# Second batch's attention spread over more steps, and a GpSimd drain behind the last gathers

## The chip, the cores and the metric

One core of one Trainium2 chip. The metric is the device time of one execution in microseconds; lower is better. The runs shown of the kernel before have a median of 853.22 us (853.07 to 855.84, 3 runs).

## The reference, cut to what matters

Four batches (b = 0 to 3), 8 heads, 576 positions of 64 features, 32 memory slots. Everything is float32 (the two weights `w_in` and `w_out` come as 64-bit floats).

```python
a = softmax(phi, axis=2)                      # over the 576 positions, per memory slot
k_m, v_m = a^T @ k, a^T @ v                   # 32 memories of each head
attn = softmax(0.125 * q @ k_m^T)             # over the 32 memories
x = merge_heads(attn @ v_m)                   # 2304 rows of 512
h = x @ w_in;  x = (h * sigmoid(h)) @ w_out   # 512 -> 2048 -> 512
# then a mixture of 8 experts, two of them for each row, weighted:
out[row] += weight * (relu(x[row] @ w1[e]) @ w2[e])
```

## The kernel before, in words

The kernel never forms `attn @ v_m`. For each batch it multiplies the memories `v_m` into `w_in` (`project`, L247: one eighth of w_in at a time for batch 0 and 1, two eighths in one call for the later batches and from index 8 on), so that the MLP's first matmul takes the attention weights as its moving operand. A large product is made of three float32r matmuls (high and low parts).

The MLP of all four batches is one list of steps, 32 for each batch (L966 and after). Step s runs `mlp_h` (L275) for one block of 128 hidden features and one of two column tiles (256 or 320 positions): six matmuls into one of two PSUM buffers "h", then tanh on ScalarE (ACT, L286), the product on VectorE (DVE, L288), and the split in high (ACT, L292) and low part (DVE, sometimes GpSimd, L293; L302 for the 64 columns left over). Four steps later `mlp_x` (L310, matmuls in L308) multiplies by w_out. All other work is hung on steps as hooks: `at(step, function, ...)`. The tile scheduler orders the instructions of each engine by the order in which the program names them and by what is ready in its own model; `tc.issue_after(i)` keeps an instruction behind `i` on its engine.

Batch 0's attention is computed ahead of the steps. During its 32 steps (about 33 to 130 us) these hooks run: `fetch_win`/`narrow_win` (turning 64-bit weights into float32 on ACT and DVE, until step 20), `fetch_wout`/`narrow_wout` (on ACT, DVE and GpSimd; block f at step 2f - 1, until step 29), `project(i)` at steps 2, 6, 10, ... 26 and the first call for batch 1, `project(8)`, at step 28; and the whole attention of batch 1:

- `phi_max` (L107), steps 8 and 9, for the two groups of four heads: maximum of phi over the positions (DVE reduction into the tile `mx`, L111, which has one buffer), a transpose on TensorE (PE, L113), a second reduction (L115), a broadcast (L117), subtraction (L120) and exp (L121).
- `memory` (L124), both groups at step 11: 40 small matmuls each (L131), then normalisation into `src` (L133 to L139).
- `memory_t` (L141) at step 14: two transposes and one copy into `kvt`.
- `scores` (L154) at steps 17 and 18, for the two column tiles: 16 matmuls each (L152) and two DVE transposes (L161).
- `softmax_a` (L163) at step 19: maximum (L167), subtraction (L168), exp (L169). `softmax_b` (L172) at step 22: sum (L176), two small instructions (L177, L178), product (L179).
- `split` (L194) at steps 24 and 26: a DVE transpose for each group (L183), high part on ACT (L190), low part on DVE (L191) into the tiles `ah` (three buffers) that `mlp_h` of step 32 reads first.

`phi_max`, `memory`, `memory_t`, `scores` and `project` take their PSUM from one tag, "aux", of two buffers, which are given out in turn; a call that needs one waits until ACT or DVE has read what was in it. `project`'s evictions are L258 (ACT) and L259 (DVE). Batches 2 and 3 do the same during the steps of the batch before them, with both `phi_max` calls ten steps in, and their reduction L111 kept behind the newest L293 on DVE.

Loads are issued by SyncE (SP) in the scheduler's order: phi (L87) goes into the buffer "big", which phi shares with the scores of the batch before; k/v (L97) and q (L105) have four buffers each, which the next batch reuses; the 64-bit weights go through `stage` (L201).

The experts come last (L723): nine parts of up to 640 rows. GpSimd gathers each part's rows by indirect DMA and scatters results into `out` (L716). For a part after the first expert the earlier values of `out` are gathered first (`earlier`, L637, DMAs in L641); for the last part (k = 8) `earlier` is all that GpSimd does ahead of five scatters. At the very end there is a branch over an overflow path (L793), and each engine drains (L1052).

Of the kernel before, what the change touches and what calls it, by code (L numbers as in the profile page):

```python
# [6 lines left out]
F32 = mybir.dt.float32  # L7
# [5 lines left out]
OP = mybir.AluOpType  # L13
AX = mybir.AxisListType

B, H, S, D, M = 4, 8, 576, 64, 32
# [3 lines left out]
SC, NCH = 128, 5  # L20
# [24 lines left out]
def body(ctx, tc, a):  # L45
    nc = tc.nc
    pe, act, dve, pool, sp = nc.tensor, nc.scalar, nc.vector, nc.gpsimd, nc.sync
# [13 lines left out]
    ident = const.tile([128, 128], F32, name="ident")  # L61
# [15 lines left out]
    ap_ = att.enter_context(tc.tile_pool(name="att", bufs=1, side="right"))  # L77
# [24 lines left out]
    def load_q(b, r, t0=0, t1=S):  # L102
        if t0 == 0:
            QT[b, r] = ap_.tile([128, S], F32, name="q", tag="q", bufs=4)
        sp.dma_start(QT[b, r][:, t0:t1], a["qt"][b, r][:, t0:t1])  # L105

    def phi_max(b, g):  # L107
        r = slice(g * 128, (g + 1) * 128)
        mx = ap_.tile([SC, 128], F32, name="mx")
        with tc.issue_after(LATEST[0].ins) if b > 1 else ExitStack():  # L110
            dve.tensor_reduce(mx, PH[b][:, :, r].rearrange("p c j -> p j c"), axis=AX.X, op=OP.max)  # L111
        pt = psum("aux", 2)
        pe.transpose(pt[:, :SC], mx, ident)  # L113
        mt = ap_.tile([128, 1], F32, name="mt")
        dve.tensor_reduce(mt, pt[:, :SC], axis=AX.X, op=OP.max)  # L115
        pb = psum("aux", 2)
        pe.matmul(pb[:SC, :128], mt.to_broadcast([128, SC]), ident, start=True, stop=True)  # L117
        for c0, c1 in ((0, 2), (2, NCH)):
            e = PH[b][:, c0:c1, r]
            dve.tensor_sub(e, e, pb[:SC, None, :128].to_broadcast([SC, c1 - c0, 128]))  # L120
            last = act.activation(e, e, AF.Exp)  # L121
        return last
# [514 lines left out]
    def earlier(k):  # L637
        for j in range(PARTS[k][2]):
            h = height(k, j)
            EX[k, j] = P2["b"].tile([128, DM], F32, name="ex", bufs=CT)[:h]  # L640
            last = pool.indirect_dma_start(out=EX[k, j], out_offset=None, in_=a["out"],  # L641
                                           in_offset=bass.IndirectOffsetOnAxis(ap=GID[k][:h, j:j + 1], axis=0))
        return last
# [79 lines left out]
    def experts(late, last):  # L723
        open_b()
        for k, (e, t0, n) in enumerate(PARTS):
            first, nxt = t0 == 0, k + 1 < len(PARTS)
            new = nxt and PARTS[k + 1][0] != e
            if first:
                for c in range(4):
                    loaded = fetch_w2(e, c)  # L730
            if k == 1:
                gather(2)
                indices(3)
            elif k and nxt:
                with tc.issue_after(puts[-1].ins):
                    g = gather(k + 1, loaded)
                with tc.issue_after(g.ins):
                    g = earlier(k)
                if k + 2 < len(PARTS):
                    with tc.issue_after(g.ins):  # L740
                        indices(k + 2)
            elif k:
                earlier(k)
            for f in range(8):
                up(k, f)
                if k == 0 and f == 2:
                    late(15, 17)
                if k == 0 and f == 4:
                    routed = last(17, 18)
                    split_w2(e, 0)  # L750
                    split_w2(e, 1)
                    table(1)
                    with tc.issue_after(gather(1).ins):
                        table(2)
                        for c in range(2):
                            W1S[1, c] = P2["b"].tile([128, FE], F32, name="w1s", bufs=2)
                            pool.memset(W1S[1, c][:, :1], 0.0)
                            fetch_w1(1, c)
                        for i in range(3, len(PARTS)):
                            table(i)  # L760
                if first and f % 2 and (k or f > 3):
                    split_w2(e, f // 2)
            if nxt:
                flips = iter(range(PARTS[k + 1][2]))
                ahead = PARTS[k + 1][2] - n
                for j in range(max(1, (ahead + 2) // 2) if k else 0):
                    with tc.issue_after(LATEST[0].ins):
                        flip(k + 1, next(flips))
            if new and k > 1:
                for c in range(2):  # L770
                    fetch_w1(e + 1, c)

            for j in range(n) if nxt else (n - 1, *range(n - 1)):
                done = down(k, j, {} if k or j < n - 1 else {10: lambda: flip(1, 0), 18: lambda: flip(1, 1)})
                if nxt and k:
                    for i in range(max(1, (ahead + 2) // 2)):
                        i = next(flips, None)
                        if i is not None:
                            with tc.issue_after(done.ins) if k > 1 else ExitStack():
                                flip(k + 1, i)  # L780
                if new and j < 4:
                    split_w1(e + 1, j)
                    if j < 2:
                        fetch_w1(e + 1, j + 2)
            if new:
                for c in range(n, 4):
                    split_w1(e + 1, c)
                    if c < 2:
                        fetch_w1(e + 1, c + 2)
# [54 lines left out]
        load_q(0, r, T0[1])  # L844
    fetch_wout(0)
    fetch_win(1)
    phi_max(0, 0)
    phi_max(0, 1)
    memory(0, 0)
    memory(0, 1)  # L850
    first = ST.pop(("i", 0))
# [30 lines left out]
    def at(s, fn, *args):  # L882
        hooks.setdefault(s, []).append((fn, args))
# [10 lines left out]
    at(8, routing_setup)  # L894
    for b in range(1, B):
        s = (b - 1) * SB
        o = 2 if b == 1 else 0
        at(s + (1 if b > 1 else 4), load_phi, b)
        for r in range(4):
            at(s + (1 if b > 1 else 5 + r), load_kv, b, r)  # L900
        for r in range(4):
            at(s + (1 if b > 1 else 10), load_q, b, r)
        x = 2 if b > 1 else 0
        at(s + x + 8, phi_max, b, 0)
        at(s + x + 9 - (b > 1), phi_max, b, 1)
        at(s + x + o + 9, memory, b, 0)
        at(s + x + o + 9, memory, b, 1)
        at(s + o + 12, memory_t, b)
        at(s + o + 15, scores, b, 0)
        at(s + o + 16, scores, b, 1)  # L910
        at(s + o + 17, softmax_a, b, 0, S)
        at(s + o + 20, softmax_b, b, 0, S)
        at(s + o + 22, split, b, 0, 0, S)
        at(s + o + 24, split, b, 1, 0, S)
        for i in range(0, NP, 2):
            for x in range(2):
                at(s + SB - 8 + 4 * i, fetch_win, b * NP + i + x)
            at(s + SB - 4 + 4 * i, project, b * NP + i, 2)
# [13 lines left out]
    s = 3 * SB  # L932
# [123 lines left out]
```

## Time and profile before

| | us |
|---|---|
| median of 3 runs | 853.22 |
| the profiled execution | 852.59 |
| its span, first to last instruction | 850.7 |
| TensorE busy | 808.0 |
| VectorE busy | 497.2 |
| ScalarE busy | 361.5 |
| GpSimd busy | 208.6 |

The profile is of one execution. PE is TensorE's matmul, PEld its weight load, DVE VectorE, ACT ScalarE, POOL GpSimd, SP SyncE; a q behind a name is the engine's sequencer (waits, branches, drains, DMA issues), whose time is not counted as busy. Times are counted from the first instruction. TensorE's granted clock was 1.00, 2.4 GHz, in all stretches shown.

### The profile page before, as it was taken

To read this page: it belongs to the slowest core of one execution; us is meant where nothing else is said; L and a number is where in the kernel's file an instruction comes from. 1 tells how busy PE (TensorE), PEld (TensorE's weight loads), DVE (VectorE), ACT (ScalarE), POOL (GpSimd) and SP (SyncE) were. 2 spreads that over 40 slices of the span, in tenths; PEclk is the share of its full clock that TensorE was granted. 3 is DMA by queue.
4 is the path that set the end of the run, shared out by engine and by line. 5 is a ranking of instruction groups with operands and counts; after the bars stand their busy time and mean duration, and the time that the engine had idled before them with its cause. 6 is when DMAs were issued, how large, how long until landed. Compare 5 with 4: busy or idle time off the path is not lost.

```text
span 850.7 us, 14185 instructions
## 1 busy us (share of the span) xinstructions
PE 808.0 (95%) x5260; PEld 691.7 (81%) x5260; DVE 497.2 (58%) x1178; ACT 361.5 (42%) x856; POOL 208.6 (25%) x237
## 2 busy tenths in 40 slices
PE   5588999999999999999999999999999999999994
PEld 2266678778887888887989989989889898898983
DVE  4898996885258757655725555354553545545520
ACT  3688875444344554553413433324333233332410
POOL 0244350021000400500542404115032141331301
PEclk9999999999999999999999999999999999999998
DMA  9899861353064315222456893766748657475201
GB/s 298 282 304 312 301 204 60 111 159 121 1 215 169 51 50 150 58 81 50 112 148 193 249 271 122 157 245 184 210 145 195 236 163 178 176 204 186 73 16 40
DMA packets 85935, 137.84 MB, mean 162 GB/s; under 512 B 14045, under 2 KB 48349, under 8 KB 85856
## 3 DMA queue, kind: packets, MB, share of 16 engines
q1 hardware_dynamic: 74656, 104.41, 40.8%
q0 software_dynamic: 11200, 32.43, 12.4%
q8 instruction: 43, 0.70, 0.4%
q14 instruction: 36, 0.29, 0.1%
HBM read 106.13 MB, written 31.26 MB: 162 GB/s over the span
## 4 chain that ended last, share of the span: by engine, by line
PE 83%; DVE 8%; ACT 3%; issue 2%; DMA 2%; POOL 1%; SPq 0%; POOLq 0%; ACTq 0%
PE x L701 25%; PE x L308 18%; PE x L677 12%; PE h L677 12%; PE h L283 9%; PE aux L152 3%; DVE gl L293 1%; DMA kv<-kv 1%; PE aux L131 1%; POOL wo L227 1%; DVE wo L212 1%; DVE th L288 1%; DMA q<-qt 1%; PE aux L654 1%; ACT lw L206 0%
## 5 line engine op out<-in xcount | busy, mean ns | idle before, releaser
L701 PE MATMUL x<-w,gh 128*128 128x512 f32 (+1 forms) x608 | 188.2, 391 | 0.0
L701 PEld LDWEIGHTS x<-w,gh 128*128 128x128 f32 (+1 forms) x608 | 112.5, 186 | 24.3
L701 PE MATMUL x<-w,gl 128*128 128x512 f32 (+1 forms) x304 | 118.6, 390 | 0.0
L677 PE MATMUL h<-xh,w 128*128 128x304 f32 (+4 forms) x512 | 118.5, 303 | 0.0
L677 PE MATMUL x<-xh,w 128*128 128x304 f32 (+4 forms) x512 | 117.9, 302 | 0.0
L283 PE MATMUL h<-ah,wph 128*128 128x320 f32 (+1 forms) x512 | 108.9, 301 | 3.6 <-DVE th L288 2.0
L308 PE MATMUL x<-gh,woh 128*128 128x512 f32 x256 | 104.8, 410 | 0.0
L283 PEld LDWEIGHTS h<-ah,wph 128*128 128x128 f32 x512 | 90.2, 192 | 17.9 <-ACT ah L190 3.6
L308 PE MATMUL x<-gh,wol 128*128 128x512 f32 x256 | 101.7, 397 | 0.0
L716 POOL DMA_INDIRECT out<-y,tab x40 | 41.6, 1041 | 244.0 <-DVE y L711 189.1
L308 PE MATMUL x<-gl,woh 128*128 128x512 f32 x256 | 100.7, 393 | 0.7 <-DVE gl L293 0.7
L492 POOL DMA_INDIRECT tab_d<-rows,slot x36 | 40.6, 1129 | 194.6 <-DVE slot L489 180.4
L288 DVE SCALAR_TENSOR_TENSOR th<-th,h 128x256 f32<-128x256 f32 (+1 forms) x128 | 57.6, 450 | 52.6 <-ACT th L286 51.9
L677 PEld LDWEIGHTS h<-xh,w 128*128 128x128 f32 x512 | 87.2, 188 | 0.7
L677 PEld LDWEIGHTS x<-xh,w 128*128 128x128 f32 x512 | 87.3, 188 | 0.0
L286 ACT ACTIVATE th<-h 128x256 f32<-128x256 f32 (+1 forms) x128 | 52.2, 408 | 70.8 <-PE h L283 68.3
L677 PE MATMUL x<-xl,w 128*128 128x304 f32 (+4 forms) x256 | 77.9, 304 | 0.0
L677 PE MATMUL h<-xl,w 128*128 128x304 f32 (+4 forms) x256 | 77.7, 303 | 0.0
L283 PE MATMUL h<-ah,wpl 128*128 128x256 f32 (+1 forms) x256 | 76.8, 301 | 0.7 <-DVE wpl L259 0.7
L292 ACT ACTIVATE gh<-th 128x256 fp32r<-128x256 f32 x128 | 53.3, 416 | 55.9 <-DVE th L288 55.7
L293 DVE TENSOR_TENSOR gl<-th,gh 128x256 fp32r<-128x256 f32 x120 | 55.9, 466 | 31.8 <-ACT gh L292 27.9
L711 DVE SCALAR_TENSOR_TENSOR y<-x,tab,ex 128x512 f32<-128x512 f32 (+2 forms) x35 | 26.2, 749 | 71.4 <-PE x L701 71.4
(189 smaller groups left out, 1344.4 us busy)
## 6 DMA issues: line engine op xcount, KB each, us to landing
w2s<-moe_w SPq DMA_DIRECT2D x32, 512.0 KB, 8.1
wi<-win_d SPq DMA_DIRECT2D x24, 512.0 KB, 4.8
w1s<-moe_w SPq DMA_DIRECT2D x24, 512.0 KB, 4.8
kv<-kv SPq DMA_DIRECT2D x16, 520.0 KB, 7.7
st<-moe_w_in SPq DMA_DIRECT2D x16, 512.0 KB, 5.6
st<-moe_w_out SPq DMA_DIRECT2D x16, 512.0 KB, 7.1
xs_d<-ex SPq DMA_DIRECT2D x25, 256.0 KB, 3.6
x_d<-xs SPq DMA_DIRECT2D x36, 128.0 KB, 2.5
```

The source lines that it names most:

```text
L152: pe.matmul(p[g][h * M:(h + 1) * M], KVT[b][r, t, h * M:(h + 1) * M], moving(h)[r], start=True, stop=True)
L283: pe.matmul(p[:, :w], wt[:, g, c:c + 128], AH[b, g][at][:, t0:t0 + w], start=(n == 0), stop=(n == 5))
L286: act.activation(th[:, :w], p[:, :w], AF.Tanh, scale=0.5)
L288: dve.scalar_tensor_tensor(u[:, :w], th[:, :w], 1.0, p[:, :w], op0=OP.add, op1=OP.mult)
L292: act.activation(gh, u[:, :256], AF.Copy)
L293: last = (pool if b == 0 and (2 * f + i) % 4 == 0 else dve).tensor_sub(gl, u[:, :256], gh.bitcast(F32))
L308: pe.matmul(X2[key], held, moved, start=(f == 0 and n == 0), stop=(f == NF - 1 and n == 2))
L492: st = pool.indirect_dma_start(out=tab_d, out_offset=bass.IndirectOffsetOnAxis(ap=slot[:, j, k:k + 1], axis=0), in_=rows.bitcast(I32)[:, j ...
L677: pe.matmul(p[:, :w], wt[:, d, c], x[:, d, r], start=(n == 0), stop=(n == 11))
L701: mm = pe.matmul(p, g, w[:, f, :], start=(n == 0), stop=(n == (15 if both else 23)))
L711: done = dve.scalar_tensor_tensor(y, p[:P], w, EX[k, j], op0=OP.mult, op1=OP.add)
L716: st = pool.indirect_dma_start(out=a["out"], out_offset=bass.IndirectOffsetOnAxis(ap=TAB[k][:P, j, 0:1], axis=0), in_=y, in_offset=None, b ...
```

## The change

Three edits. `phi_max` is cut in two: `phi_top` is the first reduction, in a tile `mx` of two buffers, and `phi_max` the rest. The hooks are placed anew: for batch 1 `phi_top` at 7 and 9, `phi_max` at 9 and 11, `memory` at 12 and 13, `memory_t` at 16, `scores` at 20 and 23, `softmax_a` at 24, `softmax_b` at 25, `split` at 27 and 28; for batches 2 and 3 only `phi_top` moves, to eight and nine steps into the batch before. GpSimd gets a `drain` instruction behind the five gathers of the last part.

```diff
-    def phi_max(b, g):
+    MX = {}
+
+    def phi_top(b, g):
         r = slice(g * 128, (g + 1) * 128)
-        mx = ap_.tile([SC, 128], F32, name="mx")
+        mx = MX[b, g] = ap_.tile([SC, 128], F32, name="mx", bufs=2)
         with tc.issue_after(LATEST[0].ins) if b > 1 else ExitStack():
             dve.tensor_reduce(mx, PH[b][:, :, r].rearrange("p c j -> p j c"), axis=AX.X, op=OP.max)
+
+    def phi_max(b, g):
+        r = slice(g * 128, (g + 1) * 128)
         pt = psum("aux", 2)
-        pe.transpose(pt[:, :SC], mx, ident)
+        pe.transpose(pt[:, :SC], MX.pop((b, g)), ident)
...
             elif k:
-                earlier(k)
+                with tc.issue_after(earlier(k).ins):
+                    pool.drain()
...
-        o = 2 if b == 1 else 0
...
-        x = 2 if b > 1 else 0
-        at(s + x + 8, phi_max, b, 0)
-        at(s + x + 9 - (b > 1), phi_max, b, 1)
-        at(s + x + o + 9, memory, b, 0)
-        at(s + x + o + 9, memory, b, 1)
-        at(s + o + 12, memory_t, b)
-        at(s + o + 15, scores, b, 0)
-        at(s + o + 16, scores, b, 1)
-        at(s + o + 17, softmax_a, b, 0, S)
-        at(s + o + 20, softmax_b, b, 0, S)
-        at(s + o + 22, split, b, 0, 0, S)
-        at(s + o + 24, split, b, 1, 0, S)
+        if b == 1:
+            for step, fn, g in ((7, phi_top, 0), (9, phi_max, 0), (9, phi_top, 1), (11, phi_max, 1),
+                                (12, memory, 0), (13, memory, 1)):
+                at(step, fn, b, g)
+            for step, fn, *more in ((16, memory_t), (20, scores, 0), (23, scores, 1), (24, softmax_a, 0, S),
+                                    (25, softmax_b, 0, S), (27, split, 0, 0, S), (28, split, 1, 0, S)):
+                at(step, fn, b, *more)
+        else:
+            at(s + 8, phi_top, b, 0)
+            at(s + 9, phi_top, b, 1)
+            at(s + 10, phi_max, b, 0)
+            at(s + 10, phi_max, b, 1)
+            at(s + 11, memory, b, 0)
+            at(s + 11, memory, b, 1)
+            at(s + 12, memory_t, b)
...
```

The lines left out at the end are the other hooks of batches 2 and 3, which stay where they were.

## Rows read from the trace of the kernel before

**Rows 1.** The page, busy us of each engine (share of the span) and instructions.

```profile
PE 808.0 (95%) x5260; PEld 691.7 (81%) x5260; DVE 497.2 (58%) x1178; ACT 361.5 (42%) x856; POOL 208.6 (25%) x237
```

**Rows 2.** Busy time by stretch: PE, PEld, DVE, ACT, POOL; then clock, DMA share, GB/s.

```profile
56.50:98.00 41.50, 35.12 (x302) 25.42 (x300) 36.29 (x74) 35.72 (x83) 18.75 (x17) 1.00 0.91 315
...
98.00:111.00 13.00, 13.00 (x84) 10.95 (x83) 12.81 (x25) 11.48 (x27) 4.76 (x5) 1.00 0.85 280
111.00:130.40 19.40, 17.95 (x134) 14.33 (x133) 16.82 (x31) 15.12 (x36) 8.42 (x8) 1.00 0.47 165
...
420.00:840.00 420.00, 419.68 (x2431) 379.66 (x2429) 201.76 (x368) 134.98 (x291) 121.55 (x130) 1.00 0.59 171
```

**Rows 3.** PE's waits, 50 to 131 us: total us, times, longest.

```profile
PE aux L152 <- DVE sct L161: 2.1, 2, 1.4
PE aux L113 <- DVE mx L111: 1.7, 1, 1.7
PE aux L144 <- DVE wpl L259: 1.4, 1, 1.4
```

**Rows 4.** Timeline of DVE: the second batch's two reductions (start, us).

```profile
47.79 1.30 DVE L111 TENSOR_REDUCE mx<-phi 128x128 f32<-128x640 f32 x1
...
60.23 1.23 DVE L111 TENSOR_REDUCE mx<-phi 128x128 f32<-128x640 f32 x1
```

**Rows 5.** Timeline of PE: the same transpose in batches 2 and 3.

```profile
159.69 0.30 PE L113 MATMUL aux<-ident,mx 128*128 128x128 f32 x1 [1.03 <-DVE rows L473]
...
255.06 0.30 PE L113 MATMUL aux<-ident,mx 128*128 128x128 f32 x1 [0.46 <-DVE mx L111]
```

**Rows 6.** Lines L1052, L793 (end) and L1047 (start): ns min/median/max, first and last start.

```profile
L1052 POOLq DRAIN  x3: 46/103/4322, 845.5 to 850.4; - x3
L1052 SPq DRAIN  x3: 7/7/13, 846.2 to 850.1; - x3
...
L793 POOLq INC_SWDGE_SEM  x1: 1235/1235/1235, 844.3 to 844.3; - x1
...
L1047 POOLq INC_SWDGE_SEM  x1: 27/27/27, 0.1 to 0.1; - x1
...
L1047 POOLq DRAIN  x1: 172/172/172, 0.3 to 0.3; - x1
```

**Rows 7.** Groups, 56.5 to 98 us: busy us, mean ns of one, idle before.

```profile
L152 PE MATMUL aux<-q,kvt 64*32 64x256 f32 (+1 forms) x32 | 2.1, 415 | 0.0
...
L161 DVE STREAM_TRANSPOSE sct<-aux 128x256 f32<-128x256 f32 (+1 forms) x4 | 1.9, 474 | 0.2 <-PE aux L152 0.2
```

**Rows 8.** Groups of DVE, 98 to 130.4 us.

```profile
L168 DVE TENSOR_TENSOR sct<-sct,smx 128x1152 f32<-128x1152 f32 x1 | 1.3, 1348 | 0.0
...
L167 DVE TENSOR_REDUCE smx<-sct 128x36 f32<-128x1152 f32 x1 | 1.3, 1341 | 0.0
L176 DVE TENSOR_REDUCE ssm<-sct 128x36 f32<-128x1152 f32 x1 | 1.3, 1339 | 0.0
...
L178 DVE RECIPROCAL ssm<-ssm 128x36 f32<-128x36 f32 x1 | 0.4, 374 | 0.0
L177 DVE TENSOR_SCALAR ssm<-ssm 128x36 f32<-128x36 f32 x1 | 0.2, 176 | 0.0
```

**Rows 9.** Timeline of ACT: the tanh of step 24.

```profile
111.10 0.37 ACT L286 ACTIVATE th<-h 128x256 f32<-128x256 f32 x1
```

**Rows 10.** SP's waits at line L87, the loads of phi (ns min/median/max).

```profile
L87 SPq EVENT_SEMAPHORE  x3: 17/1638/4035, 36.0 to 188.7; - x3
```

**Rows 11.** Timeline of POOL: last gather, first and last scatter of the last part.

```profile
800.38 0.90 POOL L641 DMA_INDIRECT ex<-out,gid  x1 [0.30 <-issue]
819.77 0.94 POOL L716 DMA_INDIRECT out<-y,tab  x1 [18.49 <-DVE y L713]
...
840.75 0.97 POOL L716 DMA_INDIRECT out<-y,tab  x1 [4.46 <-DVE y L711]
```

**Rows 12.** The chain of waits through 38 to 132 us, shares by engine and line.

```profile
by line: DVE gl L293 10.0%; issue 8.9%; PE x L308 8.8%; PE h L283 8.6%; POOL wo L227 7.5%; DVE wo L212 6.2%; DMA q<-qt 5.7%; DVE th L288 4.4%; DVE gc L302 3.3%; PE aux L152 3.2%; ACT lw L206 3.1%; DVE wi L216 3.1%; ACT gh L292 2.9%; ACT wi 
```

More of the change, by code (lines that the diff above doesn't have):

```diff
@@ L105, in load_q @@
         sp.dma_start(QT[b, r][:, t0:t1], a["qt"][b, r][:, t0:t1])
+    MX = {}
+    def phi_top(b, g):
+        r = slice(g * 128, (g + 1) * 128)
+        mx = MX[b, g] = ap_.tile([SC, 128], F32, name="mx", bufs=2)
+        with tc.issue_after(LATEST[0].ins) if b > 1 else ExitStack():
+            dve.tensor_reduce(mx, PH[b][:, :, r].rearrange("p c j -> p j c"), axis=AX.X, op=OP.max)
     def phi_max(b, g):
         r = slice(g * 128, (g + 1) * 128)
-        mx = ap_.tile([SC, 128], F32, name="mx")
-        with tc.issue_after(LATEST[0].ins) if b > 1 else ExitStack():
-            dve.tensor_reduce(mx, PH[b][:, :, r].rearrange("p c j -> p j c"), axis=AX.X, op=OP.max)
         pt = psum("aux", 2)
-        pe.transpose(pt[:, :SC], mx, ident)
+        pe.transpose(pt[:, :SC], MX.pop((b, g)), ident)
         mt = ap_.tile([128, 1], F32, name="mt")
@@ L846, in body @@
     fetch_win(1)
-    phi_max(0, 0)
-    phi_max(0, 1)
+    for g in range(2):
+        phi_top(0, g)
+        phi_max(0, g)
     memory(0, 0)
@@ L902, in body @@
             at(s + (1 if b > 1 else 10), load_q, b, r)
-        x = 2 if b > 1 else 0
-        at(s + x + 8, phi_max, b, 0)
-        at(s + x + 9 - (b > 1), phi_max, b, 1)
-        at(s + x + o + 9, memory, b, 0)
-        at(s + x + o + 9, memory, b, 1)
-        at(s + o + 12, memory_t, b)
-        at(s + o + 15, scores, b, 0)
-        at(s + o + 16, scores, b, 1)
-        at(s + o + 17, softmax_a, b, 0, S)
-        at(s + o + 20, softmax_b, b, 0, S)
-        at(s + o + 22, split, b, 0, 0, S)
-        at(s + o + 24, split, b, 1, 0, S)
+        if b == 1:
[13 more added lines that the diff above has]
+            at(s + 12, memory_t, b)
+            at(s + 15, scores, b, 0)
+            at(s + 16, scores, b, 1)
+            at(s + 17, softmax_a, b, 0, S)
+            at(s + 20, softmax_b, b, 0, S)
+            at(s + 22, split, b, 0, 0, S)
+            at(s + 24, split, b, 1, 0, S)
         for i in range(0, NP, 2):
```

## The prediction

> **What bounds the kernel now.** I read the page's busy times first: TensorE is busy for 808.0 of 850.7 us, VectorE for 497.2 [rows 1]. A gain must come from the 43 us in which TensorE stands still, or from the tail behind its last matmul. The table by stage shows where they are [rows 2]: in 420 to 840 us, the experts, TensorE is busy for 419.68 of 420.00 us, so nothing is to be had there. The first batch's MLP is different. In 56.5 to 98.0 us (about steps 8 to 18) TensorE is busy for 35.12 of 41.5 us and VectorE for 36.29; in the two stretches from 98.0 to 130.4 us (steps 19 to 31) 13.00 + 17.95 and 12.81 + 16.82 of 32.4 us. Both engines are nearly full throughout: that is the fact on which most of this turns.
>
> The waits of TensorE there [rows 3] are of one kind for the most part. The second batch's attention and the projections of w_in share the two PSUM buffers "aux". The transposed memory waits 1.39 us for the eviction of project(4) in front of it in step 14; project(5) waits 2.1 us for the transposes of the first scores. The 1.7 us at the transpose of the second phi maximum come from a tile: `mx` has one buffer, so the reduction of group 1 cannot start before the transpose of group 0 has read it. The first reduction runs at 47.79, the second only at 60.23 us [rows 4]. All waits that lie in 56.5 to 98.0, small ones with them, add up to 41.50 - 35.12 = 6.38 us.
>
> In the later batches the same transpose waits 1.03 and 0.46 us, since the reduction is issued in the step of its reader [rows 5]. At the end, the last scatter is issued at 840.75 us [rows 11], and the program ends 10 us later: GpSimd's INC_SWDGE_SEM starts at 844.3 us (1.235 us), its DRAIN follows and takes 4.322 us [rows 6]. SyncE is at its own drain by 846.3 us [rows 6] and waits.
>
> **The change part by part.** *Second batch, first stretch (steps 8 to 18).* Each pair of "aux" users is now about two steps from the next, and `mx` has two buffers. No arithmetic is added or taken away, and the first batch's own calls keep their order. Both scores leave this stretch: 32 matmuls, 2.1 us of TensorE, and 4 VectorE transposes, 1.9 us [rows 7]. That leaves 35.12 - 2.1 = 33.0 us of TensorE and 36.29 - 1.9 = 34.4 us of VectorE. Of these VectorE is the longer: the stretch can shrink from 41.5 to 34.4 us, by 7.1.
>
> *Steps 19 to 23 (98.0 to 111.0 us).* TensorE had no gap here, 13.00 of 13.00 us [rows 2], and takes in the scores: 13.0 + 2.1 less what their starts overlap, about 14.9 us. VectorE loses five softmax instructions (maximum 1.34, subtraction 1.35, sum 1.34, two small ones 0.37 + 0.18; 4.58 us in all [rows 8]) and has room. This stretch grows by 1.9 us.
>
> *Steps 24 to 31 (111.0 to 130.4 us).* Step 24's tanh is at 111.10 us [rows 9]. VectorE was busy for 16.82 of 19.4 us [rows 2] and gets those 4.58 us: 21.4 us in a stretch that TensorE could do in 17.95. It grows by 2.0 us. The work that stays beside it in VectorE's queue (narrowing w_out, evictions of project(7) and project(8)) waits behind the softmax; w_out's narrowed tiles are needed four to five steps later, which covers them, but the eviction of h is not covered by more than the two "h" buffers. ACT's one exp and two splits move along and lie beside VectorE's work.
>
> Sum for the second batch: 34.4 + 14.9 + 21.4 = 70.7 us against 41.5 + 13.0 + 19.4 = 73.9, a gain of 3.2. This takes each stretch at its longer engine, without waits. By the same rule the kernel before would need 36.29 + 13.0 + 17.95 = 67.2 us and takes 73.9, 10% more; 6.38 of those 6.7 us are the waits that the change pulls apart, so I take the bare rule. Bounds: all of TensorE's idle time in both stretches, 7.8 us, on one side; on the other each stretch keeps VectorE's share of before (87% in the first and the last): 34.4/0.874 + 14.9 + 21.4/0.867 = 79.0, a loss of 5.1.
>
> *Queues that the moves pass.* SyncE's loads for the third batch wait for buffers of the second: phi for the last turn (now two steps later; such a load waits up to 4.0 us [rows 10]), k/v for memory (one or two later), q for the scores (three to five later). Behind them in that queue stand loads of w_out and w_in. The last w_out tiles are narrowed at steps 25 to 29, well behind step 23, so I cost this at nothing, and at up to 2 us if SyncE stays blocked on q until then. By that time the DMA engines' share has fallen from 0.91 to 0.47 [rows 2], which leaves room to catch up.
>
> *Third and fourth batch.* Two reductions of 1.2 us go two and one steps ahead of their readers. TensorE's 1.03 + 0.46 us go. VectorE does the routing's small work there, and 2.5 us of it move behind the reductions; GpSimd, which waits for that routing, has idle time. Bounds: 1.5 us of gain, and none if a reduction is again queued late. I take 1.3.
>
> *The drain.* It is one instruction on GpSimd, behind five gathers that end at 801.3 us; the next instruction there is a scatter that waits for its data until 819.77, after 18.49 us of idleness [rows 11]. A drain of 4.3 us, or one that waits for those gathers to land, is hidden there; were that cover gone, it would hold up the first scatter alone, and four others stand between that and the end. What it does to the last DRAIN no row shows. The rows around it are 172 ns in front of any DMA, and 46 and 103 ns for the two that come right after the long one [rows 6]. Two readings fit: the DRAIN works off something that all the DMAs before it left behind, or it pays for whatever ran last. The first makes the last DRAIN some 0.2 us, with five scatters behind the early one. Then SyncE's end at 846.3 us sets the finish, which comes 0.8 us after it now comes (849.9 to 850.7): 847.1, a gain of 3.6 us. The other end is nothing; a loss is excluded by the 18 us. I take 3.6, because the other three DRAINs, with little or nothing new in front of them, are all short, and five scatters are few beside all that GpSimd issued before. The Trainium skill (VectorE: DVE Perf Modes, The DRAIN you can't avoid) says that the preamble's and postamble's drains take about 12 ns, constant, on all engines; by that the last DRAIN has nothing to give, and the sum would be that of the first rival. GpSimd's 4.322 us disagree with the page.
>
> **Sum.** The profiled execution took 852.59 us (span 850.7). 852.6 - 3.2 - 1.3 - 3.6 = 844.5. The median of the runs shown is 853.22, 0.6 above it, so I forecast 845.1 us.
>
> **Rivals.** *The drain moves nothing.* The last DRAIN pays for INC_SWDGE_SEM just before it, or for the last scatters, and still takes 4.3 us. For it: INC_SWDGE_SEM takes 1.235 us there and 27 ns at the start [rows 6], so the DMAs' bookkeeping may hang on it and not on the drain. Against it: the two later drains are short. Time: 845.1 + 3.6 = 848.7 us.
>
> *The attention moves nothing.* The chain of waits through 38 to 132 us runs over VectorE, ACT and GpSimd more than over TensorE [rows 12]: narrowing the 64-bit weights goes ACT, VectorE, GpSimd, ACT, VectorE. If this chain sets the pace, taking away TensorE's waits only makes it wait for the next tanh. The scheduler may also place the moved work where it was before. Against it: VectorE itself is idle for 5.2 us of the first stretch. With the drain working: 853.2 - 3.6 - 1.3 = 848.3 us; without, 851.9.
>
> *Slower: VectorE's last stretch.* The softmax is squeezed into steps 24 to 28, the attention's halves have to be ready at step 32, and TensorE waits there for evictions of h and for the halves. Its price is the lower bound above, 5.1 us less the 1.3: 853.2 + 3.8 = 857.0 us without the drain's gain. It decides if the first stretch gives back less than the 3.9 us that the other two take. Against it: 111 to 130 us is where VectorE still had 2.6 us idle.
>
> **Chances.** Forecast 0.42; drain moves nothing 0.28; attention moves nothing 0.20 (0.13 with the drain working, 0.07 without); slower 0.10. The range reaches over the forecast and the two rivals at 848: from 842 (3 us of the second batch's upper bound beyond my sum) to 852. Outside lie the slower case and the edges, about 0.2. A measurement of this kernel tells some 0.3%, 2.6 us, from no change, so the cases of 845 and 848 count as faster with a few misses, 0.77; the 851.9 and neighbours as the same, 0.13; slower 0.10.
>
> **What would show it.** TensorE's waits at the memory, its transpose, the scores and both phi transposes gone; steps 8 to 18 near 35 us long, steps 24 to 31 near 21; VectorE close to full in the last. On GpSimd a drain between 801 and 806 us, and the last DRAIN at 0.2 us. I am wrong if the last DRAIN is still 4.3 us, or if TensorE shows new waits for th or ah in steps 24 to 32 of the size of those that went.

## The result, and the profile after

The changed kernel takes 845.51 us (median of 4 runs, 844.75 to 846.22) against 854.53 us of the kernel before beside it (853.07 to 855.88, 4 runs): a ratio of 0.9887, 95% interval 0.9866 to 0.9908. The forecast was 845.1 us in a range of 842 to 852. The profiled execution takes 845.91 us (span 844.1) against 852.59: 6.7 us less, where the medians differ by 9.0. Where the other 2.3 us come from is a finding of its own (below).

First the lead along the program: the start of tanh (ACT) in some steps, the end of the last product y on VectorE, and the end of the span, from the timelines of the two profiled executions.

| | before | after | lead |
|---|---|---|---|
| step 0 | 32.58 | 32.39 | 0.2 |
| step 8 | 58.40 | 58.32 | 0.1 |
| step 19 | 98.83 | 93.69 | 5.1 |
| step 24 | 111.10 | 109.63 | 1.5 |
| step 32 | 131.58 | 129.61 | 2.0 |
| step 48 | 177.13 | 174.20 | 2.9 |
| step 80 | 272.95 | 270.37 | 2.6 |
| step 127 | 385.45 | 382.88 | 2.6 |
| last y ends | 840.47 | 838.35 | 2.1 |
| span ends | 850.71 | 844.13 | 6.6 |

So the second batch gave 2.0 - 0.2 = 1.8 us, the third 0.9, the fourth took 0.4 back, and the end behind the last y shrank from 10.24 to 5.78 us, by 4.46. The 0.4 us between step 127 and the last y belong to the execution and not to the change: in the other profiled executions below that stretch differs from the one of before by 0.0 to +2.1 us, with the attention changed or not.

The page of the changed kernel, busy us of each engine, and its stretches, cut at the same steps as those of [rows 2]:

```profile
PE 807.1 (96%) x5260; PEld 691.4 (82%) x5260; DVE 496.8 (59%) x1178; ACT 360.8 (43%) x856; POOL 209.9 (25%) x237
```

```profile
56.40:92.90 36.50, 35.12 (x284) 27.02 (x282) 32.62 (x67) 33.10 (x80) 17.75 (x17) 1.00 0.92 317
92.90:109.50 16.60, 14.88 (x114) 11.22 (x114) 14.99 (x31) 15.21 (x35) 8.65 (x9) 1.00 0.88 314
109.50:128.40 18.90, 17.61 (x132) 13.79 (x130) 18.22 (x32) 13.19 (x32) 6.76 (x6) 1.00 0.43 155
```

The busy times are those of before, as no work came or went. The three stretches take 72.0 us in place of 73.9 [rows 2]; TensorE stands for 4.39 us in them (1.38 + 1.72 + 1.29), where it stood for 7.83. PE's waits from 50 to 131 us, in the columns of [rows 3], show which ones went and which came:

```profile
PE h L288 <- DVE wpl L264: 2.3, 2, 1.2
PE aux L157 <- DVE wpl L264: 0.7, 1, 0.7
PE aux L122 <- DVE mt L120: 0.7, 1, 0.7
PE h L288 <- DVE th L293: 0.5, 1, 0.5
PE aux L136 <- ACT phi L126: 0.4, 1, 0.4
PE h L288 <- DVE ah L196: 0.3, 1, 0.3
```

The three of [rows 3] are gone. But the waits for `wpl`, the low part of the projected weights, which VectorE evicts, only moved, most of them to h. Before, beside the 1.4 us of [rows 3], there were (lines of the attention and the MLP have moved on by five since: L264 was L259, L288 was L283, L136 was L131):

```profile
PE h L283 <- DVE wpl L259: 0.7, 1, 0.7
PE aux L131 <- DVE wpl L259: 0.7, 1, 0.7
```

So they were 2.8 us before and are 2.3 + 0.7 = 3.0 after. On DVE's timeline the second reduction of phi now follows the first by 3.3 us, where it was 12.4 us [rows 4]:

```profile
47.60 1.30 DVE L113 TENSOR_REDUCE mx<-phi 128x128 f32<-128x640 f32 x1
50.90 1.33 DVE L113 TENSOR_REDUCE mx<-phi 128x128 f32<-128x640 f32 x1
```

At the end, GpSimd's drains and INC_SWDGE_SEM (columns of [rows 6]; L749 is the new drain) and its last DMAs (timeline):

```profile
L749 POOLq DRAIN  x1: 9474/9474/9474, 794.4 to 794.4; - x1
...
L799 POOLq INC_SWDGE_SEM  x1: 300/300/300, 842.3 to 842.3; - x1
...
L1067 POOLq DRAIN  x3: 46/103/464, 842.6 to 843.9; - x3
```

```profile
798.26 0.90 POOL L646 DMA_INDIRECT ex<-out,gid  x1 [0.30 <-issue]
817.65 0.94 POOL L721 DMA_INDIRECT out<-y,tab  x1 [18.49 <-DVE y L718]
...
838.63 0.97 POOL L721 DMA_INDIRECT out<-y,tab  x1 [4.47 <-DVE y L716]
```

The new drain is issued at 794.4 us, while gathers are still in front of it on the engine, and is over at 803.8; the scatter behind it waits for its data until 817.65 all the same, with the 18.49 us of idleness that [rows 11] showed. In return the last DRAIN takes 0.464 us in place of 4.322, and INC_SWDGE_SEM 0.300 in place of 1.235.

### The profile page after: what moved, and what is told of

The parts are those of the page before. It is cut to its first block, busy times and chain, and to the rows that moved or that the text cites. A ratio compares the mean times of both kernels' runs of the same rounds, so it can differ in the third digit from the quotient of the medians.

```text
span 844.1 us, 14185 instructions
## 1 busy us (share of the span) xinstructions
PE 807.1 (96%) x5260; PEld 691.4 (82%) x5260; DVE 496.8 (59%) x1178; ACT 360.8 (43%) x856; POOL 209.9 (25%) x237
## 3 DMA queue, kind: packets, MB, share of 16 engines
q1 hardware_dynamic: 74656, 104.41, 40.9%
## 4 chain that ended last, share of the span: by engine, by line
PE 81%; DVE 9%; ACT 4%; DMA 3%; issue 2%; POOL 1%; SPq 0%; POOLq 0%; ACTq 0%; DVEq 0%
PE x L706 25%; PE x L313 18%; PE x L682 13%; PE h L682 12%; PE h L288 9%; PE aux L157 2%; DMA st<-moe_w_out 1%; DVE th L293 1%; DVE gl L298 1%; DMA kx<-kx 1%; ACT lw L211 1%; POOL wo L232 1%; DMA st<-moe_w_in 1%; DVE mx L113 1%; DVE wo L217 1%
## 5 line engine op out<-in xcount | busy, mean ns | idle before, releaser
L288 PE MATMUL h<-ah,wph 128*128 128x320 f32 (+1 forms) x512 | 109.3, 302 | 3.8 <-DVE th L293 1.7
L288 PEld LDWEIGHTS h<-ah,wph 128*128 128x128 f32 x512 | 90.0, 192 | 18.2 <-ACT ah L195 3.6
L288 PE MATMUL h<-ah,wpl 128*128 128x256 f32 (+1 forms) x256 | 76.6, 300 | 2.3 <-DVE wpl L264 2.3
L298 DVE TENSOR_TENSOR gl<-th,gh 128x256 fp32r<-128x256 f32 x120 | 55.1, 459 | 32.0 <-ACT gh L297 28.1
```

The lines of the kernel that those rows point to most:

```text
L288: pe.matmul(p[:, :w], wt[:, g, c:c + 128], AH[b, g][at][:, t0:t0 + w], start=(n == 0), stop=(n == 5))
L298: last = (pool if b == 0 and (2 * f + i) % 4 == 0 else dve).tensor_sub(gl, u[:, :256], gh.bitcast(F32))
```

## The experiments

The profiled executions below start their first step 0.2 to 0.8 us sooner than before's; a lead is therefore always counted from step 0. The runs came from several chips, on which the kernel before has different times, so each is compared with the kernel before beside it.

**The two parts, each alone.** The drain without the attention's edits:

```diff
             elif k:
-                earlier(k)
+                with tc.issue_after(earlier(k).ins):
+                    pool.drain()
```

> The kernel before with the GpSimd drain alone; the attention's hooks and phi_max as they were. Theory (the drain behind the last gathers shortens the end by itself): the last y product stays where it was (840.5 us), the end behind it shrinks from 10.2 to about 5.8 us, and the time falls by about 4.5 us against the kernel before. INC_SWDGE_SEM is about 0.3 us and the last DRAIN about 0.5 us, as in the changed kernel. Rival (the end is shorter for another reason, since the scatters of the changed kernel come about 2 us earlier): the last DRAIN stays near 4.3 us and the time is that of before, or the end only shrinks by part of it.

And the attention's edits without the drain, from the changed kernel:

```diff
             elif k:
-                with tc.issue_after(earlier(k).ins):
-                    pool.drain()
+                earlier(k)
```

> The changed kernel with the GpSimd drain taken out again; all hooks of the attention as changed. Theory (the two parts add up and share nothing): the last y product comes about 2.1 us earlier than in the kernel before, the end behind it takes 10.2 us as there, and the time falls by about 2.1 us against the kernel before. Rival (the medians fell by 9.0 us, more than the two profiled executions' 6.7, so the attention is worth more than the steps show): the time falls by 4 us or more. Second rival (the attention's new places give nothing once the drain is away): within 1 us of the kernel before.

| | us | kernel before, same chip | ratio, 95% interval |
|---|---|---|---|
| drain only | 851.49 (848.78 to 852.07, 9 runs) | 856.00 (852.47 to 857.13, 14 runs) | 0.9947 [0.9928, 0.9966] |
| attention only | 849.05 (848.87 to 850.62, 6 runs) | the same | 0.9935 [0.9911, 0.9959] |

The end behind the last y is 5.78 us with the drain alone, and 10.39 with the attention alone. Their rows for the last DRAIN (drain only, then attention only):

```profile
L1053 POOLq DRAIN  x3: 46/103/464, 848.3 to 849.6; - x3
```

```profile
L1066 POOLq DRAIN  x3: 46/103/4322, 842.1 to 847.0; - x3
```

The drain alone is worth 4.5 us, as the theory had it. The attention alone was expected to give 2.1 us, and gave 7.0: the rival with "4 us or more". The two profiled executions differ by only 3.5 us, 0.8 of it from their starts. What fills the gap stands in the runs of the kernel before: 4 of the 14 lie at 852.5 to 852.7 us, the other 10 at 855.7 to 857.1. The profile of before is one of the short ones. The drain-only kernel, whose attention is that of before, parts in the same way (3 runs at 848.8 to 849.3 us, 6 at 850.8 to 852.1), and its profile, one of the longer, shows what the long ones have. PE in it, from 56.5 us on (stretch, length, PE busy, granted clock, DMA share, GB/s):

```profile
56.50:93.00 36.50, 30.12 (x266) 1.00 0.92 309
...
93.30:103.30 10.00, 10.00 (x39) 0.50 0.97 345
103.30:110.00 6.70, 6.70 (x50) 0.98 0.41 105
```

For 10 us TensorE runs at 1.2 GHz and not at 2.4, right in the steps where both engines are full. Up to step 18 this execution is 0.7 us ahead of the profile of before; from step 20 on it is 3.3 us behind: the fall costs 4.0 us. The changed kernel, the attention-only kernel and every other kernel here with the scores at steps 20 and 23 keep 1.00 there in their profiles. That the long runs of before have this fall is inferred: of a run without a profile only the mean clock is known (0.983 to 0.995 in the short runs, 0.972 to 0.990 in the long ones), but the program up to there is the same and the size fits. The mean clocks fit too, if like is compared with like. The profile of before holds no record of the clock ahead of 40.9 us and shows 1.00 there, where TensorE ran at 1.2 GHz (last section); 21 us at half the clock are 0.012 of the span, and so far apart are the two clocks among the short runs (0.983 twice, 0.995 twice, at the same times). The long runs have 0.972 to 0.974 and 0.990: lower by about 0.009 and 0.005, where a fall of 10 us makes 0.006. So the medians' 9.0 us are the profiles' 6.7, plus 1.9 by which before's median lies above its profile (2 of its 4 runs were long ones) and 0.4 by which the changed kernel's lies below its own.

**The second batch's halves.** Early half alone (memory_t and what follows back in the old steps):

```diff
-            for step, fn, *more in ((16, memory_t), (20, scores, 0), (23, scores, 1), (24, softmax_a, 0, S),
-                                    (25, softmax_b, 0, S), (27, split, 0, 0, S), (28, split, 1, 0, S)):
+            for step, fn, *more in ((14, memory_t), (17, scores, 0), (18, scores, 1), (19, softmax_a, 0, S),
+                                    (22, softmax_b, 0, S), (24, split, 0, 0, S), (26, split, 1, 0, S)):
```

> The changed kernel with the second batch's late half back in its old steps (memory_t 14, scores 17 and 18, softmax_a 19, softmax_b 22, split 24 and 26); only phi's maximum and the memory keep their new ones. Theory A (TensorE's clock falls behind its long stand at the first scores, where it waits for their transposes, as in the drain-only kernel at 93.3 us): that wait is back, about 2 us in steps 17 and 18, so some or most of the runs show the lower clock and are some 3 us longer than the rest. Theory B (what keeps the clock up is the denser work ahead of it, phi's maximum and memory): no run shows a fall behind 90 us and the times lie in one group as the changed kernel's. Time without a fall: the early half's 2.3 us at step 16 stand and half of them is lost again by step 24, 846 to 847 us; with a fall 849 to 850.

Late half alone:

```diff
-            for step, fn, g in ((7, phi_top, 0), (9, phi_max, 0), (9, phi_top, 1), (11, phi_max, 1),
-                                (12, memory, 0), (13, memory, 1)):
+            for step, fn, g in ((8, phi_top, 0), (8, phi_max, 0), (9, phi_top, 1), (9, phi_max, 1),
+                                (11, memory, 0), (11, memory, 1)):
```

> The changed kernel with the second batch's early half back in its old steps (both phi maxima whole in steps 8 and 9, though the tile keeps two buffers, memory twice in step 11); only memory_t, scores, softmax and split keep their new ones. Theory A (the clock falls behind the stand at the first scores): that stand is gone, every run has the clock of the changed kernel and the times lie in one group. Theory B (the denser early steps hold the clock up): a fall in some of the runs, as in the kernel before. Time: if each half gives what the steps show, step 16 is back where it was in the kernel before apart from what the second buffer gives, step 32 is 0 to 1 us ahead of the kernel before, and the time is 846 to 848 us.

| | us (5 runs each) | ratio to before (859.90, 857.10 to 860.77, 9 runs) | lead from step 0 to 32 |
|---|---|---|---|
| early half | 853.92 (853.30 to 854.28) | 0.9932 [0.9918, 0.9946] | -2.8 |
| late half | 852.47 (851.24 to 853.70) | 0.9918 [0.9903, 0.9933] | -0.15 |

PE's waits and stretches with the early half alone:

```profile
PE aux L157 <- DVE sct L166: 3.9, 1, 3.9
```

```profile
88.00:91.60 3.60, 0.87 (x5) 0.94 0.50 155
91.60:98.00 6.40, 5.26 (x40) 0.50 0.93 322
98.00:104.00 6.00, 6.00 (x40) 1.00 0.84 292
```

The early half wins 2.0 us by step 16, near the 2.3 expected, and more than that is lost again: TensorE comes to the first scores sooner, VectorE turns them no sooner, project(5) waits 3.9 us for a buffer where it waited 2.1 in two pieces, and in that stand the clock falls to 1.2 GHz, until 98.0 us. Theory A had the fall right, though the runs don't part into two groups; "half of them is lost again" was far too kind. With the late half alone that wait is gone and the clock stays up, with the early steps where they were, which theory B excluded:

```profile
PE h L288 <- DVE wpl L264: 2.2, 2, 1.2
PE aux L122 <- DVE mt L120: 1.6, 1, 1.6
```

```profile
92.00:98.00 6.00, 4.88 (x36) 1.00 0.90 341
```

Neither half gains in the steps (-2.8 and -0.15 us) over the profile of before, which has no fall; both together gain 1.8 to 2.4, in eight profiled executions of kernels that have both. By the medians, the drain's 4.5 us taken off, the halves are worth 1.5 and 2.9 us, since most runs of before are of the long kind. The early half is worth 2 us only when the late half has moved the place where it would be given back.

**The scores apart.** The smallest edit that should take the stand away, in the kernel before (batch 1 alone has o = 2):

```diff
-        at(s + o + 16, scores, b, 1)
-        at(s + o + 17, softmax_a, b, 0, S)
+        at(s + 16 + 2 * o, scores, b, 1)
+        at(s + 17 + 2 * o, softmax_a, b, 0, S)
```

> The kernel before with one thing moved: the second batch's second scores go from step 18 to step 20 and softmax_a from 19 to 21, so the first scores' transposes have three steps to free the buffers. No drain, phi's maximum and memory as before. Theory (TensorE's clock falls behind its stand at the first scores, and that fall makes the longer of the two groups of times of the kernel before): the wait for sct is gone, every run lies in one group near the shorter times of before, the median is 3 us or so below before's, and the last y product is within 1.5 us of the 840.5 us of before's profile, or of its like on this chip. Rival (the fall comes from something ahead of the scores): two groups of times or a fall behind 90 us remain.

857.58 us (856.99 to 859.35, 12 runs) against 859.77 (856.34 to 862.10, 17 runs), ratio 0.9981 [0.9969, 0.9994]. The theory's premise fell:

```profile
PE aux L152 <- DVE sct L161: 2.1, 2, 1.4
```

```profile
92.00:98.00 6.00, 5.30 (x36) 1.00 0.93 346
```

The wait is what it was: project(5) in step 18 waits for the first scores of step 17, and both stayed where they were. And yet the clock holds at 1.00 from 90 to 111 us in its profile, and 9 of its 12 runs lie at 857.0 to 857.9, near the short times of before on that chip (3 of 17 at 856.3 to 857.4). The other three lie at 858.7 to 859.4, and the profile is of one of them: it has a fall of its own much later, of some 3 us at 355 us, behind a wait of 2.0 us of h for VectorE's product (waits from 328 to 395 us, and the stretch):

```profile
PE h L283 <- DVE th L288: 2.0, 1, 2.0
```

```profile
354.00:360.00 6.00, 5.69 (x23) 0.72 0.01 1
```

The changed kernel on the same chip has that wait too, and keeps 1.00 (below). So the rival is right in that a fall behind 90 us remains, but it is not the one at the scores. What went from behind the stand at the scores is the second block of 16 score matmuls. So three pictures of what TensorE did before the clock fell or held: a stand of 3.9 us (fell), of 1.4 + 0.7 us with the second scores behind it (fell in the drain-only kernel's profile, held in before's), the same without them (held). Each rests on one or two profiled executions. In steps the edit costs 0.9 us (lead from step 0 to 32).

**The later batches.** Both reductions back beside their readers:

```diff
-            at(s + 8, phi_top, b, 0)
-            at(s + 9, phi_top, b, 1)
-            at(s + 10, phi_max, b, 0)
-            at(s + 10, phi_max, b, 1)
+            for g in range(2):
+                at(s + 10, phi_top, b, g)
+                at(s + 10, phi_max, b, g)
```

> The changed kernel with the third and fourth batch's first reduction back beside its reader, ten steps in; the second batch and the drain stay changed. Theory (the two batches gave +0.93 and -0.36 us): step 32 as in the changed kernel (2.0 us ahead of before, give or take where the first step starts), steps 48 to 72 lose 0.9 us of the lead, steps 80 to 127 win 0.4 us back, so the last y product comes 0.6 us later in relation to step 32. Rival (the two differences come from the second batch's changed times and not from the reductions): the steps from 32 on keep the changed kernel's lead within 0.1 us.

The transposes wait again as in [rows 5] (timeline of PE):

```profile
156.87 0.30 PE L118 MATMUL aux<-ident,mx 128*128 128x128 f32 x1 [1.03 <-DVE mx L113]
...
252.41 0.30 PE L118 MATMUL aux<-ident,mx 128*128 128x128 f32 x1 [0.45 <-DVE mx L113]
```

The lead over before changes by -0.18 us in the third batch and -0.39 in the fourth, where the changed kernel has +0.93 and -0.36. The earlier reductions are thus worth 1.1 us in the third batch and nothing in the fourth. The 0.4 us lost there are lost with the old places too; their cause was not followed up.

**Where the drain stands.** The changed kernel with its one drain moved forward (here to the third part; for the sixth it is `k == 5`):

```diff
                     g = earlier(k)
+                if k == 2:
+                    with tc.issue_after(g.ins):
+                        pool.drain()
...
-                with tc.issue_after(earlier(k).ins):
-                    pool.drain()
+                earlier(k)
```

> The changed kernel with its one drain moved forward, to behind the earlier gathers of the third of the nine parts; about 69 of some 166 GpSimd DMAs come before it and about 97 behind it. Accumulation (a DRAIN and the INC_SWDGE_SEM in front of it work off what all the DMAs since the last drain left): the two at the end take in proportion, 97/166 of 5.5 us, about 3.2 us, and the end behind the last y is some 8.3 us. First use (the first DRAIN of the program behind DMAs is long whatever came before, each later one short): the two at the end take about 0.8 us together as in the changed kernel, and the end is 5.8 us.

For a drain behind every part, the same lines without `if k == 2:`, and the changed kernel's own drain kept:

```diff
                     g = earlier(k)
+                with tc.issue_after(g.ins):
+                    pool.drain()
```

> The changed kernel with a drain behind the earlier gathers of every part from the third on, so six or seven drains with some 15 DMAs between two of them. Accumulation: beyond the landing of its last gather the first drain takes about 69/166 of 5.5 us, 2.3 us, each later one about 0.5 us, and the end behind the last y stays at 5.8 us. First use: the first drain takes some 4 to 5 us beyond its last gather, the others next to nothing, the end 5.8 us. Drains in front of a scatter that is already due would hold it up; since the experts are bound by TensorE, the last y moves by less than 1 us.

> The changed kernel with its one drain moved to behind the earlier gathers of the sixth part, so that 45 GpSimd DMAs follow it. From the changed kernel (5 DMAs behind the drain: INC_SWDGE_SEM 0.300, DRAIN 0.464 us) and the one with the drain at the third part (90 DMAs: 1.995 and 7.411 us) a straight line gives 0.0199 and 0.0817 us for each DMA. Theory (straight line): 1.10 and 3.73 us, the end behind the last y about 9.6 us. By the same line the kernel before, with 160 DMAs and no drain, stands at 52 DMAs by both times, so its count must start anew somewhere. Rival (no line, the time depends on where the drain stands): anything else, above all 0.3 and 0.5 us, or 2 and 7.4 us.

For the drain at the first gathers:

```diff
-                gather(0)
+                with tc.issue_after(gather(0).ins):
+                    pool.drain()
```

> The changed kernel with its one drain moved far forward, to behind the first gathers of rows, with 38 of the 160 GpSimd DMAs ahead of it and 122 behind. What is open is why the kernel without a drain stands at 52 on the line of DMA counts and not at 160. Theory A (the count starts anew after some 108 DMAs since the last drain or the start): 122 - 108 = 14 are left, INC_SWDGE_SEM 0.48 us and DRAIN 1.20 us. Theory B (it starts anew at a fixed place of the program, behind its 108th DMA): 1.235 and 4.322 us as in the kernel before. Theory C (it starts anew for a reason that an early drain takes away, and the line goes on): 2.63 and 10.0 us.

Their last DRAINs, with the drain at the third part, at the sixth, at the first gathers, and behind each part:

```profile
L1069 POOLq DRAIN  x3: 46/103/7411, 843.7 to 851.6; - x3
```

```profile
L1069 POOLq DRAIN  x3: 46/103/3731, 846.8 to 851.0; - x3
```

```profile
L1067 POOLq DRAIN  x3: 46/103/959, 845.2 to 846.7; - x3
```

```profile
L745 POOLq DRAIN  x6: 8036/11760/11971, 478.8 to 752.2; - x6
...
L751 POOLq DRAIN  x1: 7652/7652/7652, 793.4 to 793.4; - x1
...
L1069 POOLq DRAIN  x3: 46/103/459, 843.9 to 845.1; - x3
```

| drain | DMAs behind it (of 160) | INC_SWDGE_SEM us | last DRAIN us | end behind last y | run, us |
|---|---|---|---|---|---|
| as changed | 5 | 0.300 | 0.464 | 5.8 | 845.51 |
| at the sixth part | 45 | 1.095 | 3.731 | 9.7 | 853.09 |
| at the third part | 90 | 1.995 | 7.411 | 14.2 | 853.71 |
| at the first gathers | 122 | 0.420 | 0.959 | 6.2 | 848.76 |
| none (before) | 160 | 1.235 | 4.322 | 10.2 | 854.53 |

(The runs are from different chips; the two columns before them are not touched by that.)

The third part's result was a miss for both theories: 90 DMAs behind the drain made the end longer than no drain did. It put the line on its feet, though. From 5 and 90 DMAs, (7.411 - 0.464) / 85 = 0.0817 us of DRAIN and (1.995 - 0.300) / 85 = 0.0199 us of INC_SWDGE_SEM for each DMA; the sixth part was then expected at 3.73 and 1.10 us, and measured 3.731 and 1.095. By the same line the kernel before stands at 52 DMAs (both columns say so), and the one with the drain at the first gathers at 11: its count starts anew after 111 DMAs behind the drain, before's after 108. That is theory A but for three DMAs; theory B wanted 4.322 us again, theory C 10.0. The drain is therefore no warming-up: it works off something that each of GpSimd's DMAs leaves behind, and something else clears that after about 110 of them. The Trainium skill (DMA: Bandwidth & Descriptors, SWDGE vs HWDGE vs iDMA) has GpSimd write the descriptors of its DMAs into rings; a ring that is full and is cleared would fit, but no run here shows it.

With a drain behind each part, the drains last 7.7 to 12.0 us, and TensorE does not notice: the lead at the last y is 3.1 us, 2.5 from step 0 on. Their lengths settle nothing between the two theories: from the end of the last gather in front, the first drain, behind 69 DMAs or so, takes 10.0 us, and the second, behind 15, takes 10.0 too. Part of that is the gathers' way to memory (4.9 us from issue to landing, median); the rest is not explained. The end was expected at 5.8 us and is 8.0: the last DRAIN is 0.459, but 2.3 us more pass among the semaphore waits in front of INC_SWDGE_SEM, which is unexplained.

**The changed kernel again**, on the chip of the scores-apart kernel, with no edit:

> The changed kernel once more, unchanged, on the chip of the two kernels beside it. Expected: every run in one group, some 10 us below the median of the kernel before, 7 us below the shorter of its groups; the end behind the last y 5.8 us. If the gain were the clock's alone, it would be no faster than the kernel with the scores apart by more than the drain's 4.5 us; by the steps the third batch's earlier reductions and the second batch give 2 us more than that.

848.43 us (848.12 to 849.32, 4 runs) against 859.77: ratio 0.9875 [0.9856, 0.9894], 11.3 us less, and its longest run is 7.0 us below the shortest of before. The two parts alone gave 4.5 + 7.0 = 11.5. It is 9.2 us faster than the scores-apart kernel, so the gain is not the clock's alone. On this chip and the halves', every profiled execution loses time that those of the first chips don't: 2.2 to 2.3 us between steps 104 and 127 (3.9 in the scores-apart kernel, with its fall), around one stand of h near 350 us, and 1.4 to 2.1 us between step 127 and the last y. The stand is the same with the old and the new attention; here, from 328 to 395 us:

```profile
PE h L288 <- DVE th L293: 2.0, 1, 2.0
```

The two add up to about the 3.8 us by which the kernel before is slower there (859.8 against 856.0). Why it happens on these chips alone is not known, so no finer sum is made. No version was found that beats the changed kernel.

## Why the prediction was right, and where not

The time came out right, 845.5 for 845.1, with two terms too large, one too small, and one that was not seen. That it agrees within 0.4 us is luck in part: the terms promised 8.1 us and the two profiled executions differ by 6.7. Of the missing 1.4 us, 1.0 does not show, since 0.6 was added for the median, and the changed kernel's median lies 0.4 below its profile.

*Second batch, forecast 3.2, measured 1.8.* The step that failed is "I take the bare rule", each stretch at its longer engine without waits. The forecast lengths were 34.4, 14.9 and 21.4 us; they are 36.5, 16.6 and 18.9. In the first stretch the longer engine is TensorE with 35.12 us and not VectorE with 32.62. Its 2.1 us of scores did leave, but its queue filled with what stood behind: 74 matmuls of `mlp_x` fall into the stretch by tanh where 66 did. The second stretch is as full as forecast, 14.88 us of TensorE, but has 1.72 us of waits where it had none. The last shrank by 0.5 us instead of growing by 2.0: VectorE is busy for 18.22 us there and not for 21.4, as part of what stood beside the softmax (low parts in L298, the narrowing of w_out) is now done one stretch earlier. Over all three, the bare rule took waits that are pulled apart for waits that go. "6.38 of those 6.7 us are the waits that the change pulls apart" was a misreading of [rows 3]: its three waits are 5.2 us, and the 6.38 are TensorE's whole idle time in the first stretch. Of the 7.83 us of idle time 4.39 remain, and the waits for `wpl` are 3.0 us in place of 2.8. That VectorE, which the moves fill, evicts the projections late for that reason is likely, but no run tested it. (The lower bound's sum is 78.9, not 79.0; nothing hangs on it.)

*Third and fourth batch, forecast 1.3.* The waits of 1.03 and 0.46 us went, and the places are worth 1.1 us in the third batch and nothing in the fourth, where waits of 0.4 us for `mt` and 0.3 for `wpl` took their place (in the third one of 0.8 for `mt` came, and the lead grew all the same). The lead shows only 0.6, because of the 0.4 and 0.2 us that both batches lose with the old places too.

*The drain, forecast 3.6, measured 4.46.* The mechanism was right: of the two readings, the one that the DRAIN works off what the DMAs left, and the 18 us of idleness covered the new drain. The size was off since INC_SWDGE_SEM, in front of it, was left at 1.235 us; it shrinks with it, by 0.935 us. "All that GpSimd issued before" was wrong: without a drain the last DRAIN stands for 52 of the 160 DMAs. SyncE's drain does set the finish as forecast: it starts at 843.3 us, and the span ends 0.9 us later. The Trainium skill (VectorE: DVE Perf Modes, The DRAIN you can't avoid) has these drains at about 12 ns on all engines; GpSimd's took 0.459 to 7.411 us here.

*The queues, costed at nothing.* Right, and for a better reason than given. The scheduler put the third batch's q behind the last load of w_out by itself, so SyncE's stand on q holds up nothing but w_in's reloads (SP's waits, 30 to 135 us):

```profile
SPq L105 <- PE aux L157: 4.0, 1, 4.0
```

*The rivals.* "The drain moves nothing" fell with the drain-only kernel (ratio 0.9947). "The attention moves nothing" fell with the attention-only one (0.9935). "VectorE's last stretch": of its mechanism only 0.3 us of waits for ah show, at the end of it (the 0.5 us for th lie at 54 us, ahead of the moved work), and the stretch got shorter; a slowing came in the early-half kernel instead, at and behind the first scores (2.8 us by step 32).

*What was not seen.* The 0.6 us added "for the median" took the runs of before for one group. They are two, 3 us or so apart, and the profile, with a clock of 1.00 in all stretches shown, was of the shorter one: nothing in its rows could show the fall, but the runs could (853.07, 853.22 and 855.84). If the long runs have the fall, as inferred above, about 3.3 us of the attention's 7.0 (856.0 less the 852.7 of the short runs) are the clock's.

## What to carry to other kernels

A small stand of TensorE can cost more than its length: where the runs of a kernel fall into two groups, look for a stretch whose clock falls in one of them, and what TensorE does just ahead of it. Moving work from in front of a wait gave nothing here unless the wait was moved too; the two halves of this edit lost 2.8 us (with a fall of the clock) and 0.15 us in the steps alone and won 1.8 together. And where GpSimd issues many DMAs, put a drain into an idle stretch of it as near to the end as there is one, with few DMAs behind it; one put too early made the end 4 us longer than none.

## What the runs showed of the hardware

- GpSimd's last DRAIN and INC_SWDGE_SEM grow by 0.082 and 0.020 us for each of its DMAs since the last drain (5, 45 and 90 of them lie on one line), and start anew after 108 to 111.
- TensorE's clock fell from 2.4 to 1.2 GHz in mid-kernel behind waits of 2.1 and 3.9 us, for 10.0 and 6.4 us; behind the 2.1 us in one of two profiled executions of the same attention. Behind 2.0 us near 350 us it fell in the scores-apart kernel, for some 3 us, and held in the changed kernel on the same chip. The Trainium skill (TensorE: Matmul & The Clock Gate, Part 1: The HAM clock gate) ties the clock to how busy TensorE has been of late; that agrees with the fall in the 3.9 us stand. Why the clock falls behind such a wait in one execution and holds in another stays open here.
- A low clock costs nothing where TensorE has time to spare. From 41 to 45 us the clock is nearly back in the changed kernel's profile and still low in the attention-only kernel's (PE busy, clock, DMA share, GB/s):

```profile
41.00:45.00 4.00, 2.91 (x13) 0.95 0.88 296
```

```profile
41.00:45.00 4.00, 3.96 (x12) 0.50 0.91 282
```

TensorE is busy for 1 us more in the second, and yet step 8 comes 25.93 us behind step 0 in the first and 25.94 in the second.
- A clock of 1.00 can be a missing record. From 20 to 41 us the profile of before shows 1.00 and the changed kernel's 0.50, but the same matmul takes the same time in both (before, then changed):

```profile
L283 PE MATMUL h<-ah,wph 128*128 128x256 f32 x8 | 3.0, 457 | 0.5 <-ACT ah L190 0.5
```

```profile
L288 PE MATMUL h<-ah,wph 128*128 128x256 f32 x8 | 3.1, 458 | 0.5 <-ACT ah L195 0.5
```

From 42 to 60 us, at 2.4 GHz, it takes 291 ns (mean) in the profile of before, so that one too ran at 1.2 GHz there. Before a clock is compared between two profiles, the time of a matmul should be.
